# Windowed attention with sinks feeding a SwiGLU block: two token groups moved from TensorE transposes to the crossbar, and the sink work regrouped

## The chip, the cores and the metric

The kernel runs on one core of one Trainium2 chip. The metric is device time in microseconds (us), lower is better. A core has TensorE (matmuls; PE in the profile, PEld for its weight loads), VectorE (DVE), ScalarE (ACT), GpSimd (POOL) and SyncE (SP, which here only issues DMAs), and 16 DMA engines that serve the queues of all of them.

## The reference

```python
# q, k, v: [4 batches, 8 heads, 768 tokens, 64]; n_sink = 4, window = 128
scores = scale * q @ k.T
keep   = (pos_k < n_sink) | ((rel >= 0) & (rel < window))      # rel = pos_q - pos_k
a      = softmax(where(keep, scores, -1e9))
x      = (a @ v).transpose(0, 2, 1, 3).reshape(3072, 512)
out    = (silu(x @ w_gate) * (x @ w_val)) @ w_out              # d_ff = 1536
```

A query sees its last 128 tokens and the first 4 of its batch. All inputs are float32, and the output is float32 [3072, 512].

## The kernel before

**Groups and blocks.** The 3072 tokens are 12 *groups* of 256, three to a batch (`GC = 3`; group g is batch g // 3, part g % 3). Attention runs by group. The SwiGLU block runs by token *blocks* of `SIZES` tokens: block 0 is group 0, block 1 group 1, block 2 group 2, block 3 groups 3 and 4, block 4 groups 5 and 6, block 5 groups 7 and 8, block 6 groups 9 and 10, block 7 group 11. Softmax needs no maximum here: scores are exponentiated directly, masked by a product, and the sum comes from a column of ones behind v.

**The steps of one group.**

- *Load.* All loads are issued by GpSimd, which casts float32 to bfloat16. `load4` brings q and k with four tokens to a row, in two DMAs (L96); `load1` brings them with one token to a row, in four DMAs (L107). `load_v` brings v in two (L123). Tiles of q and k come from `natp`, 4 buffers.
- *Turn q and k*, so that the head dimension lies on partitions. `step_T` does it on TensorE: 64 small matmuls (L270) into PSUM, evicted by ScalarE (kT) and VectorE (qT) at L275. `cross_T` does it with two DMA transposes from SyncE (L304) from the tile of `load1`, one for each 128 tokens (256 KB). `NPE` is the first group turned by the crossbar; `keys` and `queries` pick the right tile.
- *Window scores* `step_S` (L334), exponentials on ScalarE (L341), mask product on VectorE (L346), twice a group for four heads each.
- *Sink scores* `step_K` (L357): queries against the four sink keys of the batch, exponential on ScalarE (L361). `step_ks` copies the sink keys into place (L314). The first group of a batch has its sinks inside its window tiles and skips this.
- *Attention times v* `step_PV` (L381), with the sinks' part against a table `vsb`, built once a batch on GpSimd by `build_vsb` (L188). VectorE divides (L386, L393).
- *Turn x*, so that the model dimension lies on partitions: `step_X` on TensorE (L417) with an eviction (L423, or L421 on ScalarE), or a DMA transpose from SyncE (L399). `NXPE` says which groups take which; before, the DMA serves groups 3 and 5 and above.

**The block.** `gate` makes 512 columns of hidden units x tokens: 8 or 4 matmuls for the gate (`pg`), a tanh on ScalarE, 8 or 4 for the value (`pv`; both L445), and two products on VectorE (L459, L460). `down` multiplies 128 tokens by the output weights (L498), ScalarE scales (L502), SyncE stores (L504).

**The order is written by hand.** Every engine works through its instructions in program order. After a prologue (groups 0 and 1, with the loads of weights), `weave` walks through a list of *units*, each a `gate` or a `down`, and puts attention steps into them: in a gate between the gate and value matmuls, in a down between its twelve matmuls. `slots((9, T(2)), ...)` means: in unit 9, do `T(2)`. The first weave has 25 units, 0 to 24: gates of blocks 0 and 1 to unit 12, downs of block 0 in 13 and 14, then the gates of block 2 (15 to 20), the downs of block 1 (21, 22) and of block 2 (23, 24). Block 3 begins in the second weave, and each later weave is one block (the last, two). `T(g)` and `C(g)` turn group g by TensorE or crossbar, and then issue the load of group g + 4 by `next_load`.

**Queues.** GpSimd issues loads in program order; in the trace a blocked load waits for the landing of the load issued eight before it. SyncE issues crossbar transposes and stores in program order, so a transpose that waits for its load holds up what stands behind it.

Of the kernel before, what the change touches and what calls it, by code (L numbers as in the profile page):

```python
# [8 lines left out]
FP32 = mybir.dt.float32  # L9
BF16 = mybir.dt.bfloat16  # L10
# [5 lines left out]
def kernel(  # L16
# [12 lines left out]
    nc = tc.nc  # L29
    P = 128  # L30
# [12 lines left out]
    SIZES = [256, 256, 256, 512, 512, 512, 512, 256]  # L43
    assert sum(SIZES) == NTOK and NG == 12 and S == 768
    OFF = [sum(SIZES[:i]) for i in range(len(SIZES))]
    NPE = 4
    NXPE = 5
    VS = 72
    FCH = [2, 2, 2, 2, 4]
    assert sum(FCH) == DFC  # L50
# [4 lines left out]
    def pool(name, bufs, psum=False):  # L55
        if psum:
            return ctx.enter_context(
                tc.tile_pool(name=name, bufs=bufs, space=bass.MemoryType.PSUM))
        return ctx.enter_context(tc.tile_pool(name=name, bufs=bufs))
# [2 lines left out]
    wpool = pool("wpool", 1)  # L62
    natp = pool("natp", 4)
    vpool = pool("vpool", 1)
    kqtp = pool("kqtp", 3)
    crossp = pool("crossp", 4)
    epool = pool("epool", 2)
    espool = pool("espool", 2)
# [11 lines left out]
    def bank(shape, dtype, name):  # L80
        return psum.tile(shape, dtype, tag="b", name=name)
# [10 lines left out]
    def load4(g):  # L92

        x = natp.tile([P, H, 4 * D], BF16, tag="kq", name="kq")
        for i, src in ((0, k), (1, q)):
            nc.gpsimd.dma_start(  # L96
                x[64 * i:64 * (i + 1)], four_tokens(src, g, slice(0, H)))
        nat[g] = x

    def load1(g):  # L100

        b, c = divmod(g, GC)
        x = natp.tile([P, 2, 2, H * D], BF16, tag="kq", name="kq")
        for j in range(2):
            t0 = c * 256 + j * P
            for i, src in ((0, k), (1, q)):
                nc.gpsimd.dma_start(  # L107
                    x[:, j, i].rearrange("p (h d) -> p h d", d=D),
                    src[b, :, t0:t0 + P].rearrange("h m d -> m h d"))
        nat[g] = x  # L110
# [17 lines left out]
    def load_gate(i):  # L128
        f0, n = sum(FCH[:i]) * P, FCH[i] * P
        for lst, w, nm in ((wgs, moe_w_gate, "wg"), (wvs, moe_w_val, "wv")):  # L130
            t = wpool.tile([P, DMC, n], BF16, tag=f"{nm}{i}", name=nm)
            nc.gpsimd.dma_start(
                t, w[:, f0:f0 + n].rearrange("(c p) f -> p c f", p=P))
            lst.append(t)
# [51 lines left out]
    def build_vsb(b):  # L186
        vsb = const.tile([P, H, D + 1], BF16, tag=f"vsb{b}", name="vsb")
        nc.gpsimd.tensor_tensor(  # L188
            vsb,
            vcf[:, b:b + 1].broadcast_to([P, H, D + 1]),  # L190
            diag_h.rearrange("q (h o) -> q h o", o=1).broadcast_to([P, H, D + 1]),
            op=ALU.mult)
        vsbs.append(vsb)
# [19 lines left out]
        pattern=[[32, NP2], [NS, 2]], channel_multiplier=-1)  # L213
    load_v(1)
    load_gate(1)
    build_vsb(0)
    for i in range(2, 5):
        load_gate(i)

    def build_masks():  # L220

# [14 lines left out]
    def A(fn, *a):  # L236
        return lambda: fn(*a)
# [54 lines left out]
    def queries(g, r, p, j, n):  # L292

        if g < NPE:
            return qTs[g][r, p, j * P:(j + n) * P]
        return cross[g][r, j:j + n, 1, p]
# [51 lines left out]
            later.append(dve)  # L348

    def step_K(g):  # L350
        b, c = divmod(g, GC)
        if c == 0:
            return
        ps = bank([P, 256], FP32, "pk")
        for p in range(NP2):

            nc.tensor.matmul(  # L357
                ps[KS * p:KS * (p + 1)], kss[b][:, p * KS:(p + 1) * KS],
                queries(g, slice(0, P), p, 0, 2), start=True, stop=True)
        es_t[g] = espool.tile([P, 256], BF16, tag="es", name="es")  # L360
        nc.scalar.activation(es_t[g], ps, AF.Exp, scale=scale)  # L361

    def step_PV(g, j, hh, act=False):
        b, c = divmod(g, GC)
        t = 2 * c + j
        if hh == 0:
            xns[g, j] = xnp.tile([P, DM], BF16, tag="xn", name="xn")
        po = bank([P, 4, D + 1], FP32, "o")
        mms = []
        if c > 0:  # L370
            mms.append((po, es_t[g][:, j * P:(j + 1) * P],
                        vsbs[b][:, 4 * hh:4 * hh + 4]))
        for hq in range(4):
            h = 4 * hh + hq
            if t > 0:
                vp = vas[g][:, 0, h, 0:D + 1] if j else vas[g - 1][:, 1, h, 0:D + 1]
                mms.append((po[:, hq], e_t[g][:, h, 256 * j:256 * j + P], vp))
            mms.append((po[:, hq], e_t[g][:, h, 256 * j + P:256 * (j + 1)],
                        vas[g][:, j, h, 0:D + 1]))
        for i, (o, l, r) in enumerate(mms):  # L380
            nc.tensor.matmul(o, l, r, start=(i == 0), stop=(i == len(mms) - 1),  # L381
                             skip_group_check=True)

        def dve():
            rcp = smallp.tile([P, 4, 1], FP32, tag="rcp", name="rcp")
            nc.vector.reciprocal(rcp, po[:, :, D:D + 1])  # L386
            if act:
                for h in range(4):
                    nc.scalar.activation(  # L389
                        xns[g, j][:, (4 * hh + h) * D:(4 * hh + h + 1) * D],  # L390
                        po[:, h, 0:D], AF.Copy, scale=rcp[:, h])
                return
            nc.vector.tensor_tensor(  # L393
                xns[g, j][:, 256 * hh:256 * (hh + 1)].rearrange(
                    "p (h d) -> p h d", h=4),
                po[:, :, 0:D], rcp.broadcast_to([P, 4, D]), op=ALU.mult)
        later.append(dve)
        if hh == 1 and (g >= NXPE or g == 3):
            later.append(lambda: nc.sync.dma_start(  # L399
                x_tile(g, j), xns[g, j], transpose=True))  # L400

# [109 lines left out]
    def gates(tb):  # L511
        return [(gate, tb, f) for f in range(0, DFC, 512 // SIZES[tb])]

    def downs(tb):
        return [(down, tb, t) for t in range(SIZES[tb] // P)]
# [6 lines left out]
    def sinks(b):  # L522
        return [lambda: later.append(A(step_ks, b))]

    def T(g):
        def last():
            step_T(g, 1)
            next_load(g)
        return [A(step_T, g, 0), last]

    def Ss(g):
        return [A(step_S, g, p2) for p2 in range(2)]

    def PVs(g):

        return [A(step_PV, g, j, hh) for hh in range(2) for j in range(2)]

    def Xs(g):
        return [A(step_X, g, j) for j in range(2)]

    def K(g):
        return A(step_K, g)
# [5 lines left out]
    def weave(us, slots):  # L548
        assert all(i < len(us) for i in slots)
        for i, (fn, tb, x) in enumerate(us):  # L550
            fn(tb, x, slots.get(i, []))
# [7 lines left out]
    def slots(*pairs):  # L559
        sl = {}  # L560
        for at, steps in pairs:
            for i, step in zip(at if isinstance(at, tuple) else (at,) * len(steps),
                               steps):
                sl.setdefault(i, []).append(step)
        return sl

    def C(g):

        def last():
            cross_T(g)  # L570
            next_load(g)
        return [last]
# [26 lines left out]
    flush()  # L599
    step_ks(0)  # L600
    step_S(1, 0)
    load4(2)
    load_v(2)
    for i in range(4):
        load_out(i)
# [8 lines left out]
    def first_PVs():  # L614
# [3 lines left out]
        for j, hh in ((0, 0), (1, 0), (0, 1), (1, 1)):  # L618
# [1 line left out]
        flush()  # L620
        later.extend(held)

    us = [g0[0], (held_gate, 0, 2), (alone, 0, 0), g0[2], *g1[0:3], g0[3], *g1[3:6], *g0[4:6],
          *downs(0), *g2, *downs(1), *downs(2)]
    weave(us, slots(
        (0, [flush, A(step_S, 1, 1), K(1), A(next_load, 1)]), (2, [first_PVs]),
        (3, [A(step_X, 1, 0), A(step_X, 1, 1, True), flush]),
        (9, T(2)), ((10, 11), Ss(2)), (11, [K(2)]),
        (12, PVs(2)[:2] + [flush]), (13, PVs(2)[2:] + [flush]), (13, C(4)),
        (14, [A(step_X, 2, 0), A(step_X, 2, 1, True), flush]),  # L630
        (15, T(3)), ((16, 17), Ss(3)), (17, sinks(1)), ((18, 18, 19, 19), PVs(3)),
        (18, C(5)), ((20, 21), Ss(4)), (21, [K(4)]),
        ((22, 22, 23, 23), PVs(4)), (24, Xs(4))))

    def pair(ga, gb, sh=0):
        s = sh
        return [((s, s + 2), Ss(ga)), (s + 2, [K(ga)]),
                ((s + 4, s + 5, s + 6, s + 7), PVs(ga)),
                ((s + 6, s + 8), Ss(gb)), (s + 8, [K(gb)]),
                ((11, 11, 12, 12) if s else (10, 11, 12, 13), PVs(gb))]  # L640

    weave(gates(3) + downs(3), slots(
        *pair(5, 6, 2), (2, C(6)), (10, C(7))))
    weave(gates(4) + downs(4), slots((0, sinks(2)), *pair(7, 8), (3, C(8)), (10, C(9)), (14, C(10))))
    weave(gates(5) + downs(5), slots((0, sinks(3)), *pair(9, 10), (10, C(11))))
    weave(gates(6) + gates(7) + downs(6) + downs(7), slots(
        ((0, 2), Ss(11)), (2, [K(11)]), ((4, 5, 6, 7), PVs(11))))


# [33 lines left out]
```

The softmax here doesn't subtract the row's maximum and nothing guards it: scores larger than these inputs give would overflow.

## Time and profile before

| What | Value |
|---|---|
| Time, median of 3 | 245.16 us (243.38 to 245.21) |
| Span of the profiled execution | 243.4 us |
| TensorE busy | 233.3 us, 96% |
| VectorE, ScalarE, GpSimd busy | 160.6, 111.2, 71.1 us |
| DMA queue of GpSimd (loads) | 68832 packets, 13.90 MB |
| DMA queue of SyncE (stores, transposes) | 29504 packets, 12.75 MB |
| Transposes on TensorE, group 2 / group 3 | 64 matmuls from 36.75 / from 53.96 us |
| First scores of group 2 / first sink scores of group 4 | 39.62 / 70.15 us |
| Block 3 begins | 81.05 us |

The profile gives busy time by engine, the span in 40 slices, the DMA queues and the groups of instructions. A "wait" is idle time of an engine with what ended it. TensorE's share counts overlapped matmuls, so its gaps are read from its list of waits and its timeline. Times in the text are from the start of the span.

### The profile page before, as it was taken

How to read it: one execution, taken by the hardware profiler on the slowest of the kernel's cores; microseconds unless marked ns; L12 is line 12 of the kernel's file. 1: busy time of each engine (PE TensorE's matmuls, PEld its weight loads, DVE VectorE, ACT ScalarE, POOL GpSimd, SP SyncE). 2: the span in 40 equal slices, each digit the busy share in tenths (PEclk: the TensorE clock that was granted, in tenths of full speed). 3: DMA queues.
4: the chain of work that ended last, by engine and by line, in shares of the span. 5: the costliest groups of instructions: out<-in, count | busy, mean ns of one | idle time of the engine just before them, and what ended most of it. 6: DMA issues, size and time to landing. Idle time of an engine off the chain costs nothing.

```text
span 243.4 us, 5177 instructions
## 1 busy us (share of the span) xinstructions
PE 233.3 (96%) x2060; PEld 136.1 (56%) x2073; DVE 160.6 (66%) x336; ACT 111.2 (46%) x221; POOL 71.1 (29%) x92
## 2 busy tenths in 40 slices
PE   7779999999999999999999999999999999999994
PEld 2557887767755445554455454445454445488443
DVE  2688878929983489890598981399970489878100
ACT  2628637447471274532566512556612562232111
POOL 8985387794276814308000000000000000000000
PEclk9979999999999999999999999999999999999999
DMA  7999999999999999959930335900524200200132
GB/s 138 160 183 198 203 191 203 165 145 171 157 149 159 203 182 117 133 109 134 233 67 1 71 61 141 165 0 1 81 51 129 89 0 0 46 0 3 47 126 88
DMA packets 98792, 27.37 MB, mean 112 GB/s; under 512 B 84816, under 2 KB 95824, under 8 KB 98768
## 3 DMA queue, kind: packets, MB, share of 16 engines
q0 software_dynamic: 68832, 13.90, 70.2%
q1 hardware_dynamic: 29504, 12.75, 26.1%
q10 hardware_dynamic: 432, 0.39, 0.5%
q8 instruction: 16, 0.26, 0.4%
q14 instruction: 8, 0.07, 0.1%
HBM read 28.34 MB, written 6.29 MB: 142 GB/s over the span
## 4 chain that ended last, share of the span: by engine, by line
PE 87%; ACT 5%; DVE 5%; DMA 1%; issue 1%; DVEq 0%; ACTq 0%
PE pv L445 25%; PE pd L498 24%; PE pg L445 23%; PE o L381 5%; PE s L334 3%; ACT e L341 3%; PE pt L270 3%; DVE e L346 2%; PE wm L248 2%; DVE ht L460 1%; PE px L417 1%; DMA out_dram<-ot 1%; ACT xn L389 1%; DVE u L459 1%; ACT kT L275 0%
## 5 line engine op out<-in xcount | busy, mean ns | idle before, releaser
L445 PE MATMUL pv<-xT,wv 128*128 128x256 bf16 (+1 forms) x384 | 74.3, 326 | 0.9 <-DVE ht L460 0.9
L445 PE MATMUL pg<-xT,wg 128*128 128x256 bf16 (+1 forms) x384 | 74.2, 326 | 0.0
L452 ACT ACTIVATE th<-pg 128x512 f32<-128x512 f32 x72 | 43.7, 607 | 60.0 <-PE pg L445 59.4
L459 DVE SCALAR_TENSOR_TENSOR u<-th,pg 128x512 bf16<-128x512 f32 x72 | 49.2, 684 | 30.6 <-ACT th L452 30.1
L498 PE MATMUL pd<-wo,ht 128*128 128x512 bf16 x264 | 62.3, 379 | 0.6
L460 DVE TENSOR_TENSOR ht<-u,pv 128x512 bf16<-128x512 bf16 x72 | 49.5, 688 | 9.5 <-PE pv L445 2.9
L445 PEld LDWEIGHTS <-wg 128*128 128x128 bf16 x384 | 37.4, 98 | 25.4 <-issue 0.2
L341 ACT ACTIVATE e<-s 128x512 bf16<-128x512 f32 (+1 forms) x96 | 46.1, 582 | 0.9 <-PE s L334 0.8
L445 PEld LDWEIGHTS <-wv 128*128 128x128 bf16 x384 | 34.5, 97 | 21.0 <-issue 2.9
L498 PEld LDWEIGHTS <-ht 128*128 128x128 bf16 x276 | 25.8, 98 | 28.0 <-issue 0.2
L502 ACT ACTIVATE ot<-pd 128x512 f32<-128x512 f32 x23 | 13.7, 597 | 53.5 <-PE pd L498 53.5
L346 DVE TENSOR_TENSOR e<-e,mask 128x1024 bf16<-128x1024 bf16 (+1 forms) x48 | 30.4, 671 | 1.1 <-ACT e L341 0.9
L123 POOL DMA_DIRECT2D va<-in_v_dram x24 | 21.3, 894 | 6.0 <-DMA kq<-in_q_dram 3.3
L393 DVE TENSOR_TENSOR xn<-o,rcp 128x256 bf16<-128x256 f32 x46 | 19.5, 425 | 2.8 <-DMA xT<-xn 1.3
L107 POOL DMA_DIRECT2D kq<-in_k_dram x16 | 14.2, 887 | 23.8 <-DMA kqT<-kq 19.8
L381 PEld LDWEIGHTS <-e 128*128 128x128 bf16 x352 | 16.6, 98 | 7.9 <-DVE e L346 2.5
L381 PE MATMUL o<-va,e 128*128 128x65 bf16 x352 | 18.1, 195 | 2.2 <-DVE e L346 2.2
L107 POOL DMA_DIRECT2D kq<-in_q_dram x16 | 14.2, 888 | 6.4 <-DMA va<-in_v_dram 2.8
L386 DVE RECIPROCAL rcp<-o 128x4 f32<-128x4 f32 x48 | 8.4, 176 | 7.2 <-PE o L381 7.2
L275 DVE CAST qT<-pt 128x512 bf16<-128x512 f32 x7 | 4.6, 688 | 9.4 <-PE pt L270 9.4
L483 DVE TENSOR_SCALAR ot<-pd 128x256 f32<-128x256 f32 x1 | 0.4, 425 | 14.4 <-DMA out_dram<-ot 14.4
L381 PE MATMUL o<-vsb,es 128*128 128x260 bf16 x32 | 8.8, 275 | 0.8 <-ACT es L361 0.7
(61 smaller groups left out, 109.4 us busy)
## 6 DMA issues: line engine op xcount, KB each, us to landing
out_dram<-ot SPq DMA_DIRECT2D x23, 256.0 KB
va<-in_v_dram POOLq DMA_DIRECT2D x24, 128.0 KB, 9.1
kq<-in_k_dram POOLq DMA_DIRECT2D x18, 128.0 KB, 8.9
kq<-in_q_dram POOLq DMA_DIRECT2D x16, 128.0 KB, 9.2
wo<-in_moe_w_out_dram POOLq DMA_DIRECT2D x4, 384.0 KB, 12.4
wg<-in_moe_w_gate_dram POOLq DMA_DIRECT2D x4, 256.0 KB, 8.2
wv<-in_moe_w_val_dram POOLq DMA_DIRECT2D x4, 256.0 KB, 8.8
kq<-in_k_dram POOLq DMA_DIRECT2D x3, 256.0 KB, 9.0
```

The costliest lines, as they stand in the source:

```text
L107: nc.gpsimd.dma_start(x[:, j, i].rearrange("p (h d) -> p h d", d=D), src[b, :, t0:t0 + P].rearrange("h m d -> m h d"))
L123: nc.gpsimd.dma_start(va[:, j, :, 0:D], v[b, :, t0:t0 + P].rearrange("h m d -> m h d"))
L341: nc.scalar.activation(e_t[g][:, h0 + h, lo:512], pss[2 * pp + h][:, lo:512], AF.Exp, scale=scale)
L346: nc.vector.tensor_tensor(e, e, m[:, :, lo:512].broadcast_to([P, 2, 512 - lo]), op=ALU.mult)
L381: nc.tensor.matmul(o, l, r, start=(i == 0), stop=(i == len(mms) - 1), skip_group_check=True)
L393: nc.vector.tensor_tensor(xns[g, j][:, 256 * hh:256 * (hh + 1)].rearrange("p (h d) -> p h d", h=4), po[:, :, 0:D], rcp.broadcast_to([P, 4, ...
L445: nc.tensor.matmul(ps[:, i * n:(i + 1) * n], ws[fi][:, c, fo * P:(fo + 1) * P], x[:, 0:n // P, c], start=(c == 0), stop=(c == DMC - 1))
L452: nc.scalar.activation(th, pg, AF.Tanh, scale=0.5)
L459: nc.vector.scalar_tensor_tensor(u, th, 1.0, pg, op0=ALU.add, op1=ALU.mult)
L460: nc.vector.tensor_tensor(hts[tb][:, f:f + two].rearrange("p a n -> p (a n)"), u, pv, op=ALU.mult)
L498: nc.tensor.matmul(po, hts[tb][:, f, ts * P:(ts + 1) * P], wos[f // n][:, f % n], start=(f == 0), stop=(f == DFC - 1))
L502: nc.scalar.activation(ot, po, AF.Copy, scale=0.5)
```

## The change

Groups 2 and 3 are turned by the crossbar instead of TensorE (`NPE` 4 to 2): they are loaded by `load1`, `kqtp` needs only two buffers, and their `C` steps stand in units 2 and 8. X of group 4 goes through the DMA too (`NXPE` 5 to 3, so all groups from 3 on). The sink scores of the second and third group of a batch are made in one run, with one exponential over 512 columns. The first `vsb` table is built after all gate weights have been asked for instead of between them. The first weave is put in another order: the downs of block 1 (now units 15, 16) stand ahead of the gates of block 2 (now 17 to 22). It is for taking transposes off TensorE, and small operations off ScalarE.

```diff
-    NPE = 4
-    NXPE = 5
+    NPE = 2
+    NXPE = 3
...
-    kqtp = pool("kqtp", 3)
+    kqtp = pool("kqtp", 2)
...
     load_gate(1)
-    build_vsb(0)
     for i in range(2, 5):
         load_gate(i)
+    build_vsb(0)
...
     def step_K(g):
+
+
         b, c = divmod(g, GC)
-        if c == 0:
-            return
-        ps = bank([P, 256], FP32, "pk")
-        for p in range(NP2):
-
-            nc.tensor.matmul(
-                ps[KS * p:KS * (p + 1)], kss[b][:, p * KS:(p + 1) * KS],
-                queries(g, slice(0, P), p, 0, 2), start=True, stop=True)
-        es_t[g] = espool.tile([P, 256], BF16, tag="es", name="es")
-        nc.scalar.activation(es_t[g], ps, AF.Exp, scale=scale)
+        n = 1 if g < GC else GC - c
+        ps = bank([P, n, 256], FP32, "pk")
+        for i in range(n):
+            for p in range(NP2):
+
+                nc.tensor.matmul(
+                    ps[KS * p:KS * (p + 1), i], kss[b][:, p * KS:(p + 1) * KS],
+                    queries(g + i, slice(0, P), p, 0, 2), start=True, stop=True)
+        es = espool.tile([P, 2, 256], BF16, tag="es", name="es")
+        nc.scalar.activation(es[:, 0:n], ps, AF.Exp, scale=scale)
+        for i in range(n):
+            es_t[g + i] = es[:, i]
...
-        if hh == 1 and (g >= NXPE or g == 3):
+        if hh == 1 and g >= NXPE:
...
-    load4(2)
+    load1(2)
...
-    us = [g0[0], (held_gate, 0, 2), (alone, 0, 0), g0[2], *g1[0:3], g0[3], *g1[3:6], *g0[4:6],
-          *downs(0), *g2, *downs(1), *downs(2)]
+    us = [g0[0], (held_gate, 0, 2), (alone, 0, 0), g0[2], *g1[0:3], g0[3], *g1[3:6],
+          *g0[4:6], *downs(0), *downs(1), *g2, *downs(2)]
     weave(us, slots(
         (0, [flush, A(step_S, 1, 1), K(1), A(next_load, 1)]), (2, [first_PVs]),
-        (3, [A(step_X, 1, 0), A(step_X, 1, 1, True), flush]),
-        (9, T(2)), ((10, 11), Ss(2)), (11, [K(2)]),
-        (12, PVs(2)[:2] + [flush]), (13, PVs(2)[2:] + [flush]), (13, C(4)),
-        (14, [A(step_X, 2, 0), A(step_X, 2, 1, True), flush]),
-        (15, T(3)), ((16, 17), Ss(3)), (17, sinks(1)), ((18, 18, 19, 19), PVs(3)),
-        (18, C(5)), ((20, 21), Ss(4)), (21, [K(4)]),
-        ((22, 22, 23, 23), PVs(4)), (24, Xs(4))))
+        (2, C(2)), (3, [A(step_X, 1, 0), A(step_X, 1, 1, True), flush]), (8, C(3)),
+        ((11, 12), Ss(2)), (11, [K(2)]), (13, PVs(2)[:2] + [flush]),
+        (14, PVs(2)[2:] + [flush]), (14, C(4)),
+        (15, [A(step_X, 2, 0), A(step_X, 2, 1, True), flush]),
+        (15, C(5)), ((16, 17), Ss(3)), (17, sinks(1)), ((18, 18, 19, 19), PVs(3)),
+        ((19, 20), Ss(4)), (20, [K(4)]), ((21, 21, 22, 22), PVs(4))))
```

In the later weaves `K(7)` and `K(10)` stand for two groups each, and the `C` steps of groups 8, 9, 10 and 11 stand earlier:

```diff
-        return [((s, s + 2), Ss(ga)), (s + 2, [K(ga)]),
-                ((s + 4, s + 5, s + 6, s + 7), PVs(ga)),
-                ((s + 6, s + 8), Ss(gb)), (s + 8, [K(gb)]),
+        return [((s, s + 2), Ss(ga)), ((s + 4, s + 5, s + 6, s + 7), PVs(ga)),
+                ((s + 6, s + 8), Ss(gb)),
...
     weave(gates(3) + downs(3), slots(
-        *pair(5, 6, 2), (2, C(6)), (10, C(7))))
-    weave(gates(4) + downs(4), slots((0, sinks(2)), *pair(7, 8), (3, C(8)), (10, C(9)), (14, C(10))))
-    weave(gates(5) + downs(5), slots((0, sinks(3)), *pair(9, 10), (10, C(11))))
+        *pair(5, 6, 2), (2, C(6)), (10, C(7)), (14, C(8))))
+    weave(gates(4) + downs(4), slots(
+        (0, sinks(2)), *pair(7, 8), (2, [K(7)]), (5, C(9)), (10, C(10)), (14, C(11))))
+    weave(gates(5) + downs(5), slots(
+        (0, sinks(3)), *pair(9, 10), (6, [K(10)])))
     weave(gates(6) + gates(7) + downs(6) + downs(7), slots(
-        ((0, 2), Ss(11)), (2, [K(11)]), ((4, 5, 6, 7), PVs(11))))
+        ((0, 2), Ss(11)), ((4, 5, 6, 7), PVs(11))))
```

## The prediction

> **What bounds the kernel now.** I read the page first: busy time by engine, then the slices.
>
> ```profile
> PE 233.3 (96%) x2060; PEld 136.1 (56%) x2073; DVE 160.6 (66%) x336; ACT 111.2 (46%) x221; POOL 71.1 (29%) x92
> ...
> PE   7779999999999999999999999999999999999994
> ...
> DMA  7999999999999999959930335900524200200132
> ```
>
> Two resources are full: TensorE from the fourth slice to the end, and the 16 DMA engines from the second slice to about 97 us (a slice is 6.1 us). TensorE sets the end. Next, what TensorE waited for between 26 and 238 us (total, times, longest):
>
> ```profile
> PE pv L445 <- DVE ht L460: 0.9, 3, 0.4
> PE o L381 <- ACT es L361: 0.4, 1, 0.4
> PE px L417 <- ACT xn L389: 0.2, 1, 0.2
> ```
>
> That is 1.5 us, and no DMA is in it. So work taken off TensorE is won in full, but any DMA that comes late is a new stall in full: nothing later has slack to make it good. Third, the GpSimd timeline (start, duration, then idle time and who ended it):
>
> ```profile
> 31.25 0.77 POOL L141 DMA_DIRECT2D wo<-in_moe_w_out_dram  x1 [2.08 <-DMA wv<-in_moe_w_val_dram]
> ...
> 59.12 0.87 POOL L123 DMA_DIRECT2D va<-in_v_dram  x1 [1.98 <-DMA kq<-in_q_dram]
> 61.01 0.87 POOL L107 DMA_DIRECT2D kq<-in_k_dram  x1 [1.01 <-DMA kqT<-kq]
> ...
> 94.51 0.87 POOL L107 DMA_DIRECT2D kq<-in_k_dram  x1 [8.34 <-DMA kqT<-kq]
> ...
> 110.24 0.88 POOL L107 DMA_DIRECT2D kq<-in_k_dram  x1 [10.48 <-DMA kqT<-kq]
> ```
>
> A blocked load waits for the load issued eight earlier, so these rows date landings: the last gate weight at 31.2 us, q and k of group 5 at 59.1, the crossbar pairs of groups 4, 6 and 7 at 61.0, 94.5 and 110.2. When those pairs were issued stands in the SyncE timeline:
>
> ```profile
> 49.10 5.13 SPq L304 DMA_TRANSPOSE kqT<-kq  x2
> ...
> 82.14 5.67 SPq L304 DMA_TRANSPOSE kqT<-kq  x2
> ...
> 105.20 2.63 SPq L304 DMA_TRANSPOSE kqT<-kq  x2
> ```
>
> So a pair (two halves of 256 KB) takes 11.9 and 12.4 us while loads run, and 5.0 us when they don't. The DMA view says why; first 46 to 52 us (loads alone), then 87 to 93 us (loads beside a pair); columns are packets, MB, share:
>
> ```profile
> q0 software_dynamic: 7220, 0.91, 242.5%
> ```
>
> ```profile
> q0 software_dynamic: 3309, 0.42, 107.0%
> q1 hardware_dynamic: 2097, 0.53, 66.9%
> ```
>
> Loads alone: 7220/6 = 1203 packets a us, so a q, k or v load of 1024 packets takes 0.85 us. Beside a pair: 551 a us. A pair is 2048 packets at 350 a us = 5.9 us of moving, in which loads lose 54%, or 3.2 us.
>
> [...] of two mask products of 0.56 us that took 2.46 us together from 11.42, 1.3 is the length of the table built on GpSimd from 12.16 (1.30 us).
>
> **The change, part by part.**
>
> *TensorE work removed.* The transposes of groups 2 and 3 are two rows of the chain, 64 matmuls in 1.02 us each: 2.0 us. Group 4's X transposes are two pieces of 0.22 us plus 0.05 of issue: 0.5 us. Sum 2.5 us, all on the bound engine. Their evictions (four ACT casts of 0.587, four DVE casts of 0.688, two DVE copies of 0.425) lie beside TensorE and count nothing.
>
> *Sink scores of two groups in one run.* Same matmuls; three exponentials of 0.445 us fewer, three made twice as wide (about 0.6 us by the 512-column rows of ACT). ACT is 46% busy: nothing. But it adds a wait: the run for groups 4 and 5 in unit 20 reads queries of group 5, whose pair used to be wanted only in the next weave. All later matmuls are queued behind it.
>
> *First sink table behind the gate loads.* It leaves 12.16, where it holds up mask products that TensorE awaits (waits of 0.86 and 1.10 us there): 1.2 us won in the prologue. It then runs after the last gate load, issued at 17.84 for 0.74 us: 18.6 to 19.9. The mask products of group 1 stand at 19.24 and 20.22, or 1.2 earlier in the new order, so about 1 us of it collides again. TensorE needs the table at 22.96: in time. Net gain 0.2 (0 to 1.2).
>
> *Loads.* Groups 2 and 3 arrive in four loads of 1024 packets (3.4 us) instead of two that took 1.46 us each or a little less (waits at 44.38 and 45.84): +0.7 us of DMA a group.
>
> *Crossbar, group 2.* The last gate weight lands at 31.2; first halves of q and k at 31.2 + 1.7 = 32.9, all at 34.6. Pair in 11.9 us, the busy price, since v and the output weights are queued: 44.8. Low end: second half at 34.6 with the quiet pair's price less its own issue, 38.3. High end: one-for-one turns with output weights, which no row shows, 48. I take 44.8. TensorE wants it at 40.3: unit 11 starts its gate at 41.05 now, less 1.02 for the transposes, less 0.55 for a score run moved behind it, plus 0.87 of gate. Stall 4.5 us.
>
> *Crossbar, groups 3 to 5.* Loads without transposes: 34.6 + 1.7 (v) + 8.0 (output weights, 2.0 to 2.1 each by the waits at 41.05 and 43.16) = 44.3; group 3 to 47.7, v, group 4 to 52.8, v, group 5 to 57.9. The same sum for the kernel before gives 56.5, plus 2 for its overlap with one pair, 58.5 against 59.1 measured. The pairs of 2 and 3 add 3.2 each, part of pair 4 adds 2, an output store about 1: group 5 lands near 67. On the crossbar: half of group 3 is in at 44.3 + 3.2 + 1.7 = 49.2; packets follow some 3 us later, 52.3. From 52 to 69 us before, two pairs and two stores took 17 us, 8.5 a pair. Three pairs from 52.3: 77.8; at 5.9 each: 70.0. I take 76 for the pair of group 5.
>
> *What TensorE wants of them.* Without stalls unit 16 wants group 3 at 55.1, unit 19 group 4 at 63, and unit 20 the two-group sink run at 66. After the first stall, group 3 is about in time and group 4 about 1 us late. Group 5 isn't: the run waits until 76. This absorbs the earlier stalls, and the 2.5 us saved.
>
> *To the next weave.* After that run: value matmul 0.9, units 21 and 22 2 x 2.5, two downs of 2.6: 11.2 us. X of group 4 is issued 5.2 us ahead of its use, an X pair being half the packets of a q-k pair: 6 to 7 us when busy (half of 11.9), 3 when quiet. Stall 1.3 (0 to 4). Block 3 begins at 76 + 11.2 + 1.3 = 88.5 instead of 81.05: +7.5 us. From there both kernels do the same work; DMA falls idle later, but it had 8 and 10 us of slack there (waits at 94.51 and 110.24). 245.2 + 7.5 = **252.7 us**.
>
> **Rivals.**
> *A, all is hidden.* Pairs move at the quiet price: for it, DMA is not waited for at all now. Against it, two measured pairs beside loads. Time 245.2 - 2.5 - 0.2 = 242.5, down to 241.5 with the full prologue gain.
> *B, only group 2 comes late.* Stall 4.5 at unit 11, after which the crossbar keeps up (pair 5 by about 70, X hidden): +4.5 - 2.5 = +2.0, 247.2 us. For it: the lower bound of 70.0 against a want of 66 + 4.5.
> *C, group 2 pays one-for-one turns with the weights* and each later pair 9 us: pair 5 at 80, X stall 3: +13, 258 us.
> *D, the sink table* as new bound: at most 1 us, inside all the cases.
>
> **How the numbers follow.** Forecast 0.55, A 0.12, B 0.25, C 0.08. The range leaves out A and C: low 243.5, just under B with its stall at 1 us; high 257.5, pair 5 at 78 and an X stall of 4 (78 + 11.2 + 4 = 93.2, +12.2). Within 1% (242.7 to 247.6) lie the tops of A and the lower half of B, 0.12; faster 0.10; slower 0.78.
>
> **What would show it.** Right: TensorE waits in the page's first list on DMA kqT<-kq at the scores of group 2 (about 4 us near 40) and at the sink run of unit 20 (some 7 us, ending near 76), one or two us on xT at block 3; no L270 rows near 37 and 54; mask products at 11.42 back to 0.56 us and one near 19 doubled; GpSimd table at 18.6. Wrong: the score and sink matmuls of groups 2 to 5 start without idle time, or pairs in the first 70 us land within 5 to 7 us of issue.

## The result, and the profile after

The changed kernel takes 262.56 us (median of 4) against 245.19: a ratio of 1.0716, 95% interval 1.064 to 1.0793. It is slower, as forecast, but by 17.4 us where 7.5 were forecast, and 262.6 lies above the range. Span for span it is 260.8 against 243.4 us.

The page of the kernel after, the lines that answer to those of before and the slices of the granted TensorE clock:

```profile
PE 234.3 (90%) x1925; PEld 134.6 (52%) x1937; DVE 156.6 (60%) x330; ACT 109.3 (42%) x214; POOL 75.0 (29%) x96
...
PE   7698990699969929999998999999999999999994
...
PEclk9999997599997998999999999999999999999999
DMA  8999999999999999992799134460031310200132
```

TensorE has holes in the slices near 45 and 95 us (a slice is now 6.5 us), and the clock falls in the slices at and after holes, to 7 and 5 tenths near 45 us and to 7 and 8 later: these are two costs, not one. Section 4 of the page gives the shares of the chain of work that ended last, first before, then after:

```profile
PE 87%; ACT 5%; DVE 5%; DMA 1%; issue 1%; DVEq 0%; ACTq 0%
```

```profile
PE 59%; DMA 31%; POOL 3%; issue 2%; DVE 2%; SPq 1%; ACT 0%; POOLq 0%; ACTq 0%; DVEq 0%
```

From 18.7 to 78.6 us the new chain runs through loads and, at its end, the crossbar pair of group 5; TensorE isn't on it. The list of what TensorE waited for, over the whole span this time (total, times, longest):

```profile
PE s L334 <- DMA kqT<-kq: 8.6, 2, 6.0
PE pg L449 <- DMA xT<-xn: 4.8, 1, 4.8
PE pk L359 <- DMA kqT<-kq: 3.1, 2, 2.2
```

Before, there was no DMA in this list after the prologue. Where the waits stand is in the TensorE timeline (start, duration; idle time before and who ended it last):

```profile
44.91 0.29 PE L334 MATMUL s<-kqT,kT 64*128 64x128 bf16 x2 [6.05 <-DMA kqT<-kq]
47.76 0.50 PE L334 MATMUL s<-kqT 64*128 64x256 bf16 x4 [2.56 <-DMA kqT<-kq]
...
78.56 0.29 PE L359 MATMUL pk<-kqT,ks 128*32 128x256 bf16 x4 [2.16 <-DMA kqT<-kq]
...
96.40 1.51 PE L449 MATMUL pg<-xT,wg 128*128 128x512 bf16 x4 [4.85 <-DMA xT<-xn]
...
140.56 0.29 PE L359 MATMUL pk<-kqT,ks 128*32 128x256 bf16 x4 [0.94 <-DMA kqT<-kq]
```

The two halves of group 2; the sink run that wants group 5; block 3, which wants X of group 4; and, in block 4, the sink run of groups 7 and 8. Windows of the same trace (busy us and instructions of PE, PEld, DVE, ACT, POOL, then granted clock, DMA share, GB/s) show what follows the first four:

```profile
48.00:53.00 5.00, 5.00 (x42) 3.05 (x38) 1.89 (x3) 2.76 (x6) 4.91 (x6) 0.56 2.78 153
53.00:60.00 7.00, 6.89 (x68) 4.31 (x67) 4.90 (x13) 2.74 (x6) 3.36 (x5) 1.00 1.70 121
78.00:84.00 6.00, 5.44 (x49) 4.41 (x50) 3.01 (x6) 1.42 (x3) 2.33 (x3) 0.72 1.75 200
...
96.00:101.00 5.00, 4.60 (x14) 1.83 (x15) 1.38 (x2) 0.72 (x2) 0.00 (x0) 0.66 1.60 200
```

TensorE is busy there, but at 0.56, 0.72 and 0.66 of its clock: 5 x 0.44 + 6 x 0.28 + 5 x 0.34 = 5.6 us of work lost. After the wait of 6.05 us the clock was 0.50 between 44.9 and 48 us, and a wait of 2.16 us was enough to be followed by 0.72. The kernel before has such a stretch too, in its prologue. After waits of 0.86 and 1.10 us, which the table's collision with the mask products causes (two of 0.56 us take 2.46 us together while GpSimd builds it; run 4 moves the table alone, and the mask product is back at 0.56), 32 transposes take 1.07 us there (first fence) and 0.64 after the change (second fence), and the clock over 6 to 31 us averages 0.93 (0.57 over 14 to 18 us):

```profile
13.94 0.69 PE L381 MATMUL o<-va,e 128*128 128x65 bf16 x10 [1.10 <-DVE e L346]
14.56 1.07 PE L270 MATMUL pt<-ident,kq 64*64 64x64 bf16 x32
```

```profile
12.71 0.64 PE L270 MATMUL pt<-ident,kq 64*64 64x64 bf16 x32
```

The account up to block 3, which begins at 96.40 instead of 80.89 us by the timelines (+15.5): waits 6.05 + 2.56 + 2.16 + 4.85 = 15.6; slow clock 2.2 + 1.7 = 3.9; TensorE work removed -2.5; prologue -1.45 (the gate of unit 4 starts at 25.60 instead of 27.05, although a new wait of 1.14 us for value weights lies ahead of it). Sum 15.6. After block 3, 164.4 against 162.5 us: the slow clock of 1.7 there and the 0.94 us wait, less some gaps.

Why group 2 is so late, in the SyncE timeline and the DMA view for 36 to 44 us (packets, MB, share):

```profile
32.60 22.01 SPq L304 DMA_TRANSPOSE kqT<-kq  x4
```

```profile
q0 software_dynamic: 1450, 1.20, 92.6%
q1 hardware_dynamic: 1318, 0.33, 32.2%
```

The first half is issued at 32.60, as foreseen (32.9), but the second is usable only at 47.76: 15.2 us. Between 36 and 44 us load and transpose packets go nearly one for one, and a load packet carries 1.20/1450 = 830 bytes, a transposed one 250. So transposes move at 165 packets a us, where the kernel before moved 350 beside q, k and v loads (3309 packets with 0.42 MB, some 130 bytes each). It looks as if the output weights, in their large packets, set the pace of the crossbar; run 8 tests it.

### The profile page after: what moved, and what is told of

Its sections match the earlier page's. It is cut to its first block, busy times and chain, and to the rows that moved or that the text cites. A ratio compares the mean times of both kernels' runs of the same rounds, so it can differ in the third digit from the quotient of the medians.

```text
span 260.8 us, 4915 instructions
## 1 busy us (share of the span) xinstructions
PE 234.3 (90%) x1925; PEld 134.6 (52%) x1937; DVE 156.6 (60%) x330; ACT 109.3 (42%) x214; POOL 75.0 (29%) x96
## 4 chain that ended last, share of the span: by engine, by line
PE 59%; DMA 31%; POOL 3%; issue 2%; DVE 2%; SPq 1%; ACT 0%; POOLq 0%; ACTq 0%; DVEq 0%
PE pv L449 19%; PE pg L449 18%; PE pd L502 16%; DMA kq<-in_q_dram 9%; DMA kqT<-kq 6%; DMA kq<-in_k_dram 5%; DMA wo<-in_moe_w_out_dram 5%; PE o L385 4%; DMA wv<-in_moe_w_val_dram 3%; DMA xT<-xn 3%; PE s L334 2%; DMA out_dram<-ot 1%; POOL va L123 1%; POOL wg L132 1%; POOL kq L96 1%
## 5 line engine op out<-in xcount | busy, mean ns | idle before, releaser
L449 PE MATMUL pg<-xT,wg 128*128 128x256 bf16 (+1 forms) x384 | 76.7, 334 | 4.8 <-DMA xT<-xn 4.8
L449 PE MATMUL pv<-xT,wv 128*128 128x256 bf16 (+1 forms) x384 | 76.3, 333 | 1.3 <-DMA wv<-in_moe_w_val_dram 1.1
L449 PEld LDWEIGHTS <-wg 128*128 128x128 bf16 x384 | 38.3, 100 | 31.8 <-issue 6.6
L449 PEld LDWEIGHTS <-wv 128*128 128x128 bf16 x384 | 35.1, 100 | 22.8 <-issue 3.7
L346 DVE TENSOR_TENSOR e<-e,mask 128x1024 bf16<-128x1024 bf16 (+1 forms) x48 | 29.8, 656 | 6.3 <-ACT e L341 6.2
L107 POOL DMA_DIRECT2D kq<-in_k_dram x20 | 17.9, 895 | 31.8 <-DMA kqT<-kq 26.6
L107 POOL DMA_DIRECT2D kq<-in_q_dram x20 | 17.8, 889 | 7.7 <-DMA va<-in_v_dram 2.3
L334 PE MATMUL s<-kqT 64*128 64x256 bf16 (+1 forms) x208 | 12.1, 242 | 2.9 <-DMA kqT<-kq 2.6
L334 PEld LDWEIGHTS <-kqT 64*128 64x128 bf16 x208 | 7.0, 95 | 9.1 <-issue 8.7
```

Of the source, the lines that this page charges most:

```text
L107: nc.gpsimd.dma_start(x[:, j, i].rearrange("p (h d) -> p h d", d=D), src[b, :, t0:t0 + P].rearrange("h m d -> m h d"))
L334: nc.tensor.matmul(pss[2 * pp + h][:, col:col + n * P], keys(b, t, r, p), queries(g, r, p, j, n), start=True, stop=True)
L346: nc.vector.tensor_tensor(e, e, m[:, :, lo:512].broadcast_to([P, 2, 512 - lo]), op=ALU.mult)
L449: nc.tensor.matmul(ps[:, i * n:(i + 1) * n], ws[fi][:, c, fo * P:(fo + 1) * P], x[:, 0:n // P, c], start=(c == 0), stop=(c == DMC - 1))
```

## The experiments

The theory after the result, **M**: each part sends a transfer into DMA engines that are full (90% busy or more in each slice from the second) until about 117 us (the eighteenth slice); each is wanted before it can land, and TensorE stands still and then runs slowly. Its rivals are named with the runs. All times are medians; ratios are to the kernel before in the same job. The rows come from several jobs, so two of them differ clearly only where their intervals don't overlap.

| Run | What it holds | us | Ratio (95%) |
|---|---|---|---|
| after | everything | 262.56 | 1.0716 (1.064 to 1.0793) |
| a_fill | everything, with filler | 264.53 | 1.0780 (1.0758 to 1.0803) |
| a_k1 | all but two-group sink runs | 260.63 | 1.0672 (1.0625 to 1.072) |
| a_x4pe | all but X of group 4 by DMA | 259.63 | 1.0628 (1.0583 to 1.0673) |
| a_xk | crossbar for 2 and 3, order, table | 253.26 | 1.0347 (1.0305 to 1.0388) |
| a_l1pe | finer loads, X, sink runs, order, table | 257.52 | 1.0495 (1.0475 to 1.0514) |
| a_t23 | X, sink runs, order, table | 253.01 | 1.0322 (1.0286 to 1.0358) |
| xk_fill | a_xk, with filler | 252.01 | 1.0288 (1.022 to 1.0356) |
| xk_wo1 | a_xk, one of four loads of output weights | 250.14 | 1.0210 (1.0144 to 1.0276) |
| o_x4 | X, order, table | 252.15 | 1.0298 (1.0219 to 1.0378) |
| o_k2 | sink runs, order, table | 249.39 | 1.0171 (1.0085 to 1.0256) |
| xk_t2 | crossbar for 3 alone, order, table | 247.28 | 1.0107 (1.0054 to 1.016) |
| xk_t2xn | xk_t2, with five xn buffers | 244.50 | 0.9986 (0.997 to 1.0002) |
| o_l1 | finer loads, order, table | 244.22 | 0.9995 (0.9972 to 1.0018) |
| a_ord | order, table | 244.83 | 1.0003 (0.9983 to 1.0022) |
| b_table | table alone, order of before | 244.08 | 0.9951 (0.9938 to 0.9963) |

**1. Groups 2 and 3 back on TensorE (a_t23).**

```diff
-    NPE = 2
+    NPE = 4
-    load1(2)
+    load4(2)
-        (2, C(2)), ... (8, C(3)),
+        (9, T(2)), ... (15, T(3)),
```

> The change with groups 2 and 3 put back on TensorE (T(2) in unit 9, T(3) in unit 15, loads in two DMAs); order of units, two-group sink runs, X of group 4 through the DMA and the moved table kept. Theory M (the crossbar pairs of groups 2 and 3, in the middle of the loads, come late and push every later pair back): the 8.6 us of waits at the scores of group 2 vanish, pair 5 lands near 69 instead of 78.5, a small wait is left at the sink run of unit 20 (0 to 2 us) and at block 3 (1 to 3 us); 246 to 251 us. Theory R1 (it is the new order of the units and slots): no gain, 260 us or more.

Measured 253.01 us. The waits at the scores of group 2 are gone, and the sink run waits 1.55 us instead of 2.16, but block 3 still waits 5.26 us for X. Better than R1 allows, worse than M said: the crossbar pairs with their finer loads are about half of the loss, not nearly all of it.

**2. Finer loads without the crossbar (a_l1pe).** As run 1, with `load1` for groups 2 and 3 and 16 matmuls of 128x128 a group on TensorE.

```diff
+                    nc.tensor.matmul(
+                        pts[i][:, p, j * P:(j + 1) * P],
+                        nat[g][:, j, i, c:c + P], ident, start=True, stop=True)
```

> As the run before, but groups 2 and 3 are still loaded with one token to a row in four DMAs of 1024 packets each, and TensorE turns them with 16 matmuls of 128x128 a group. It tells the crossbar pairs apart from the finer loads. Theory M: within 1.5 us of the run before, 246 to 252 us. Theory R2 (the finer loads, 4096 packets a group instead of 1024, fill the DMA engines and are the cause): most of the loss stays, 257 us or more.

Measured 257.52 us, 4.5 above run 1, at the lower edge of R2: the finer loads cost something here (the other matmuls that turn them don't: with the same matmuls run 9 has 244.22 us). The sink run waits 3.76 us instead of 1.55 for the pair of group 5, and starts at 71.80 instead of 69.17. Run 9 shows the other side of this.

**3. Filler where TensorE waits (a_fill).**

```diff
-        ((11, 12), Ss(2)), (11, [K(2)]), ...
+        (11, [A(warm, 38)]), ((11, 12), Ss(2)), (11, [K(2)]), ...
-        ((19, 20), Ss(4)), (20, [K(4)]), ...
+        ((19, 20), Ss(4)), (20, [A(warm, 9), K(4)]), ...
+    warm(21)   # ahead of block 3
```

> The change with filler matmuls on zeros placed where TensorE waits: 38 ahead of the scores of group 2, 9 ahead of the sink run of unit 20, 21 ahead of block 3. The waits themselves stay; only the idle time is filled. Theory C (after idle time TensorE is granted about half its clock for some microseconds; the trace has 0.50 to 0.72 in three stretches after the waits, worth some 5.6 us): 257 to 259 us. Rival (the slow matmuls there have another cause, or filler work only pushes the rest back): 262 us or more.

Measured 264.53 us: not faster. (Its interval overlaps that of the change, so slower isn't shown.) The mean clock rose from 0.967 to 0.991 as meant, yet its timeline has nearly the same instants as above:

```profile
48.20 0.34 PE L334 MATMUL s<-kqT 64*128 64x256 bf16 x4 [1.31 <-DMA kqT<-kq]
...
79.39 0.29 PE L359 MATMUL pk<-kqT,ks 128*32 128x256 bf16 x4 [2.33 <-DMA kqT<-kq]
96.83 1.02 PE L449 MATMUL pg<-xT,wg 128*128 128x512 bf16 x4 [1.54 <-DMA xT<-xn]
```

48.2, 79.4 and 96.8 against 47.8, 78.6 and 96.4. The work that was won back ran into the next wait: the DMA engines set these instants, as the chain says, and a quicker TensorE only waits longer (2.33 instead of 2.16 us at the sink run). The last instant should still have left the 1.7 us of clock at block 3; the sink run of groups 7 and 8 took it (it waited 2.68 us instead of 0.94, and the four us from 142 us on ran at 0.57 of the clock).

**4. The table alone (b_table)**, on the kernel before.

```diff
-    build_vsb(0)
     for i in range(2, 5):
         load_gate(i)
+    build_vsb(0)
```

> The kernel before with one edit of the change alone: the first sink table is built behind all gate weight loads. Theory P (it stood in the way of the mask products of group 0, and TensorE is the bound from there on): mask products at 11.4 take 0.56 us each, the first gate starts 1.2 to 1.6 us earlier, 243.5 to 244.1 us. Rival (the collision moves to the mask products of group 1 and gives it back): 244.8 to 245.3 us.

Measured 244.08 us, ratio 0.9951 (0.9938 to 0.9963): 1.1 us faster. The gain is small, but its interval lies clear of 1, and no other run beats both kernels clearly. In its VectorE timeline the mask product of group 0 that had been held up takes its own time again; the table stands later on GpSimd:

```profile
11.77 0.56 DVE L346 TENSOR_TENSOR e<-e,mask 128x768 bf16<-128x768 bf16 x1 [0.21 <-ACT e L341]
```

```profile
18.61 1.07 POOL L188 TENSOR_TENSOR vsb<-vcf,diag_h 128x520 bf16<-128x520 f32 x1
```

The rival's collision doesn't show in this trace: the mask products of group 1 take 0.69 us each. In the kernel after one of them does (1.38 us at 17.98), but TensorE waits for none of them there. The half clock of the prologue is gone too in this trace: 1.00 over 14 to 18 us, where the kernel before has 0.57. (Three of its five executions have a mean clock of 0.99, so it may come there too.) How the 1.1 us divide between the stall and the clock behind it, no run shows.

**5. One part of the change undone, and both (a_x4pe, a_k1, a_xk).**

```diff
-        if hh == 1 and g >= NXPE:
+        if hh == 1 and (g >= 5 or g == 3):      # a_x4pe and a_xk, with
+        (24, Xs(4))                             # Xs(4) in unit 24
-        n = 1 if g < GC else GC - c
+        (one group in each run, in the slots of before)   # a_k1 and a_xk
```

> The change with one part undone: X of group 4 is turned by TensorE again (two times four transposes in unit 24). Theory M (waits stand in series, so one removed is won): the wait of 4.85 us at block 3 and the slow clock after it (1.9 us over the first three projections) go, 0.5 us of TensorE comes back: 255 to 258.5 us. Theory S (the instants are set by the DMA engines, and the wait only moves to the next transfer, as with the filler): 261 us or more.

> The change with another part undone: sink scores of one group in a run, so unit 20 wants group 4 alone, and the sink runs of groups 5, 8 and 11 stand two units or more later, as before. Theory M: the 2.2 us wait at unit 20 with its slow clock (1.6 us) and the 0.9 us wait in block 4 go; X of group 4 is issued earlier, and its wait at block 3 shrinks to 2 to 4 us: 255 to 258 us. Theory S: X of group 4 waits on the DMA engines as before and block 3 begins no earlier: 260.5 us or more.

> Both parts undone together; the crossbar for groups 2 and 3, their finer loads, the order of units and the moved table stay. Theory M: only the 8.6 us at the scores of group 2 are left, with slow clock after them; block 3 begins near 88 us: 250 to 253 us. Theory S: 257 us or more.

Measured 259.63, 260.63 and 253.26 us: 2.9 and 1.9 us won by one part, 9.3 by both. The intervals of the first two overlap that of the change, so these two gains aren't clear. It is clear that both parts together win more than the sum of the two. The first lies between the two theories, the second is S, the third just above M. With X of group 4 on TensorE, the wait at block 3 was gone, but in the list of waits the sink runs took 4.8 us instead of 3.1, the second one, in block 4, 2.69 instead of 0.94:

```profile
PE pk L359 <- DMA kqT<-kq: 4.8, 2, 2.7
```

With single sink runs, X of group 4 was still late: block 3 waited 5.66 us. So waits in series were not won one by one here: what one gave up the next partly took. With both parts gone, TensorE waits for no DMA behind the scores of group 2.

**6. Only the order of units, and the table (a_ord).**

> Only the order of units and slots of the change, and the moved table: groups 2 and 3 and X of group 4 on TensorE, one sink group a run. Theory M: no wait on a DMA is left, as fast as the kernel before with the table moved: 243.5 to 245 us. Theory R1 (the order itself costs): 248 us or more.

Measured 244.83 us, ratio 1.0003: R1 falls. TensorE has no wait on a crossbar or X transfer left. But the gain of run 4 isn't in it: by the two ratios (1.0003 and 0.9951, from two jobs, with intervals that don't overlap) the order costs about 1.3 us. Where, no run shows. Against it, the parts by themselves:

**7. X of group 4 through the DMA, and two-group sink runs, each alone on that order (o_x4, o_k2).**

> The order of units and slots of the change with groups 2 and 3 on TensorE and one sink group a run, and X of group 4 through the DMA: what that part costs by itself. Theory M (an X pair issued 5 us ahead lands later than wanted while loads still run): a wait of 1 to 4 us at block 3 and slow clock after it, 246.5 to 250 us. Rival (without the crossbar pairs of groups 2 and 3 it lands in time): 243.5 to 245.3 us.

> The same with X of group 4 on TensorE and the sink runs of two groups: what that part costs by itself. Theory M: waits of 1 to 2.5 us in unit 20 for the pair of group 5, and of about 1 us in block 4 for group 8, with slow clock: 246.5 to 248.5 us. Rival (pair 5 is in time without the pairs of groups 2 and 3): 243.5 to 245.5 us.

Measured 252.15 us (7.3 above run 6, and above M's range) and 249.39 us (4.6 above run 6, and above M's range too, though its interval, 247.4 to 251.5 us, reaches into it). X alone (timeline of o_x4):

```profile
86.18 1.86 PE L445 MATMUL pg<-xT,wg 128*128 128x512 bf16 x4 [5.91 <-DMA xT<-xn]
```

Its four projections take 1.86 us where 1.03 is usual: a wait of 5.9 us and then slow clock, without any crossbar pair for groups 2 and 3. The halves of X were issued at 77.59 and 78.87 and wanted at 80.27, and the second took 7.3 us. So they were issued 2.7 and 1.4 us ahead, not 5. The sink runs alone (timeline of o_k2):

```profile
69.51 0.29 PE L359 MATMUL pk<-kqT,ks 128*32 128x256 bf16 x4 [1.05 <-DMA kqT<-kq]
...
125.33 0.29 PE L359 MATMUL pk<-kqT,ks 128*32 128x256 bf16 x4 [2.64 <-DMA kqT<-kq]
```

The larger wait is in block 4, long after the first loads: group 8's pair stands in unit 14 of block 3, is issued at 113.09, right behind two stores on SyncE, takes 12.2 us, and is wanted at 122.7, soon after block 4 begins. Together X and sink runs cost 8.2 us (run 1), less than 7.3 + 4.6, which the intervals only just show; the wait in block 4 is 1.18 us there.

**8. Filler, and fewer output weights, where only group 2 is late (xk_fill, xk_wo1)**, both on a_xk.

```diff
+        (11, [A(warm, 40)]),                    # xk_fill
+        if i:                                   # xk_wo1, in load_out
+            wos.append(wos[0])
+            return
```

> The same base, with 40 filler matmuls ahead of the scores of group 2, the only place left where TensorE waits long. Theory C (the slow clock after a wait is a cost of its own, and here no later wait takes it back): block 3 begins about 2 us earlier, 250.5 to 251.8 us. Rival: 252.8 us or more.

> The run with X of group 4 on TensorE and one sink group a run, but only the first of the four output-weight loads is made; the downs use that one chunk for all four (the output weights of hidden units 384 to 1535 are left out of the result). It takes 3 x 2 us of loads with large packets from beside the pair of group 2. Theory M ([...] large packets hold it longest): the pair of group 2 takes 12 us as beside q, k and v loads instead of 15, the wait at its scores falls from 9.2 to 5 to 7 us: 248.5 to 251.5 us. Rival X (the crossbar or its issue sets the 15 us by itself): the wait stays at 8.5 us or more, 252.5 us or more.

With filler 252.01 us instead of 253.26, within neither range, and the intervals overlap; but the traces agree on the sign and the size: block 3 begins at 87.10 instead of 88.90. So by the traces the slow clock was a cost of its own, 1.8 us here, where no later wait took it back; by the times alone this isn't clear. Without three of four output-weight loads 250.14 us, in M's range; the timeline of xk_wo1:

```profile
40.46 0.23 PE L337 MATMUL s<-kqT,kT 64*128 64x128 bf16 x2 [1.72 <-DMA kqT<-kq]
43.92 0.51 PE L337 MATMUL s<-kqT 64*128 64x256 bf16 x4 [3.23 <-DMA kqT<-kq]
```

Issued at 32.49, usable at 43.92: 11.4 us instead of 15.1 in its base, and 2107 transpose packets moved between 36 and 44 us instead of 1209. Rival X falls: the pair's time depended on what was loaded beside it. The run takes away the large packets and their bytes together, so it doesn't tell the size of the packets from the amount.

**9. The crossbar part divided (xk_t2, o_l1, xk_t2xn).**

> Order of the change, X of group 4 on TensorE, one sink group a run; group 2 on TensorE with its two loads, group 3 alone on the crossbar. Theory M2 (nearly all of the 8 us is group 2's pair, which has the least time between landing and use): a wait of 0 to 2 us at the scores of group 3, 244 to 247 us. Rival M3 (each pair costs about half, by pushing pairs 4 and 5 back): 248 us or more.

> Order of the change, X of group 4 and groups 2 and 3 on TensorE, one sink group a run, but groups 2 and 3 loaded in four DMAs of 1024 packets each. Theory L0 (finer loads cost the DMA engines 1 to 2 us, which nothing waits for here): 244 to 246 us. Rival L1 (they alone make pairs 4 and 5 late): 247 us or more.

Finer loads alone: 244.22 us, nothing (L0). Group 3 alone on the crossbar: 247.28 us, between M2 and M3. Its trace (of the slowest of its executions, 249.75 us) has 1.5 us at the scores of group 3 and a wait that no theory had named, first on VectorE, then on TensorE:

```profile
78.70 0.42 DVE L393 TENSOR_TENSOR xn<-o,rcp 128x256 bf16<-128x256 f32 x1 [4.30 <-DMA xT<-xn]
```

```profile
80.57 2.74 PE L498 MATMUL pd<-wo,ht 128*128 128x512 bf16 x6 [3.66 <-DVE ht L460]
```

X of group 3 is issued at 69.72, behind a crossbar pair (63.20) and two stores on SyncE, and keeps its `xn` buffers (tiles with the divided attention output, from which X is turned); the division of group 4 waits for one until 78.70, in order on VectorE; the block's product stands behind it. So with more buffers:

```diff
-    xnp = pool("xnp", 3)
+    xnp = pool("xnp", 5)
```

> Group 3 alone on the crossbar as before, with five xn buffers instead of three. Theory B (the late X transpose of group 3 keeps xn buffers, the division of group 4 on VectorE waits for one, and TensorE for the product behind it): that wait goes, 244.5 to 246.3 us. Rival (the pair of group 3 itself costs the time): 246.8 us or more.

Measured 244.50 us, ratio 0.9986 (0.997 to 1.0002): theory B. Its trace, again of the slowest execution (246.39 us), has neither wait any more; 1.86 us at the scores of group 3 are left. With the buffers, group 3's pair costs nothing that can be measured, and wins nothing either, though it takes 1.0 us of transposes off TensorE. Most of the crossbar part is group 2's: 253.26 - 247.28 = 6.0 of 8.4 us. The kernel before waits for such a buffer too (1.3 us on VectorE). With the whole change five buffers weren't tried; its trace has no wait of this kind.

## Why the prediction was right and wrong

- **The bound, and the side.** Right: TensorE had no slack before, and late transfers came in as waits, one after the other. Rival A (all hidden) and rival B (only group 2 late) fell. Rival C, which had 0.08, came nearest with 258 us.
- **TensorE work removed, 2.5 us.** The account to block 3 closes with it, but no run shows it by itself, and the 1.0 us of group 3 won nothing that can be measured (run 9).
- **The table, net 0.2 (0 to 1.2).** By itself it won 1.1 us (run 4), inside the range; the collision that I charged 1 us for cost TensorE nothing. I read the waits of 0.86 and 1.10 us there and not the half clock behind them, so the trace of before held a term that the forecast lacks. In the changed kernel the gain is lost in later waits.
- **The pair of group 2: 44.8 taken, 48 as high end.** Measured 47.76. The one-for-one turns with the output weights that I set aside as rival C, since no row showed them, were nearly the case between 36 and 44 us (1450 load packets to 1318 transposed ones), and without most of these loads the pair took 11.4 us (run 8). The wait was 8.6 instead of 4.5 us.
- **The pair of group 5 at 76.** Measured 78.56; a good part of the extra wait before was absorbed here, as the prediction said. The loads of group 5 were in near 70 us instead of 67, and the pair took 8.3 us from there by the chain.
- **From there to block 3, 11.2 us plus 1.3 for X.** This is where it failed. The work took 13.0 us (78.56 to 91.55), since 1.7 were lost to the slow clock, a term that the prediction did not have at all (with filler, at full clock, it took 11.4). And X waited 4.85 where I had allowed 0 to 4. Its price was only a little low: 8.7 us from the first issue and 7.4 from the second, where I had 6 to 7. The larger error is how far ahead it is issued: I had counted 5.2 us, the length of the two downs. Its halves were issued at 87.71, when VectorE had divided (87.68), and at 89.00, and wanted at 91.55, so it had 3.8 and 2.6 us.
- **"From there both kernels do the same work."** Wrong by 1.9 us: slow clock after the last big wait, and the sink run of groups 7 and 8, which I had dismissed with the slack of the loads. Its pair is issued behind stores on SyncE, at 130.07, and takes 10.5 us.

In the forecast's own sum: 2.5 (pair 5) + 1.8 (work after it) + 3.5 (X) + 1.9 (after block 3) = 9.7, the difference between 7.5 and 17.4 but for 0.2. The mechanism was right: late transfers that come in as waits. The landing of pair 5 and the wait for X were too small, and the slow clock and the sink run of groups 7 and 8 were put at nothing.

## What to carry to other kernels

Work moved from a full engine to full DMA engines wasn't free here but late: for each moved transfer, set the time to its landing in the same traffic (here 10.5 to 15.2 us a pair among loads, 5.0 when quiet) against the instant at which it is wanted, and count everything that queues behind it or holds a buffer for it. Waits that hang on the same stretch of DMA must be judged together: undone singly, two parts here gave 2.9 and 1.9 us, together 9.3. And put a term for the slow clock, here about 1.7 us, behind every new TensorE wait of 3.2 us or more (all twelve here led to half clock), and as a possible cost behind one of 1.8 to 2.7 us (five of eight did), unless another wait follows that takes it back.

## What the runs showed of the hardware that was not expected

- A pair of crossbar transposes took 15.2 us beside loads with packets of some 830 bytes, 11.4 us with most of those loads left out, and 5.0 us in a quiet stretch. Beside the large packets transposes moved at 165 packets a us, beside packets of some 130 bytes at 350. The size of the other queue's packets fits all this; apart from their amount it wasn't tested.
- The length of a wait alone didn't decide on the clock behind it. In the traces here all twelve TensorE waits of 3.2 us and more led to half clock: projections of 1.03 to 1.05 us took up to 1.86 to 1.92 behind eleven of them, and six down matmuls of 1.47 us took 2.74 behind the twelfth (xk_t2). Of the eight waits of 1.8 to 2.7 us that began at full clock, five did (2.64 us in o_k2 and 2.68 us in a_fill, for two), each at a loss of 1.7 us, and three did not (2.69 us in a_x4pe and 2.33 us in a_fill, for two). And in o_l1 the clock over 14 to 18 us was 0.57, with no wait of more than 0.53 us since 8 us.
